# Moving half of the k and r transposes from TensorE to VectorE and DMA, with three changes to the early schedule of a recurrent-attention and SwiGLU kernel

## Chip, cores and metric

The kernel runs on one core of one Trainium2 chip, in fp32. The metric is device time in microseconds (us) of one execution, as a median over executions; lower is better. The kernel was already tuned: it takes 655.0 us, with TensorE busy for 98% of the span.

The three calls of experiments ran on three chips of the same kind (12, 8 and 2 on record). The chip of the first pair of runs is not on record; it is called the first chip below. Each call has fresh runs of the kernel before on its own chip, so times are always judged against runs of their own chip. Marks inside the traces are compared across chips too. All runs used here are in the fast state.

## The reference

Attention of the RWKV-5 kind for 4 batches, 8 heads, 768 steps and a head size of 48, followed by a SwiGLU feed-forward over 3072 tokens (384 to 1536 to 384):

```python
for t in range(S):                                   # r, k, v: (4, 8, 768, 48)
    cur = np.einsum('bhd,bhe->bhde', u[None] * kt, vt)
    y[:, :, t] = np.einsum('bhd,bhde->bhe', rt, state + cur)
    state = w[None, :, :, None] * state + np.einsum('bhd,bhe->bhde', kt, vt)
x = y.transpose(0, 2, 1, 3).reshape(B * S, H * D)    # (3072, 384)
g = x @ w_gate
out = (g * sigmoid(g) * (x @ w_val)) @ w_out
```

## The kernel before

The kernel treats attention in 24 **units** of 128 steps (six chunks of four batches). For each unit, k and r are multiplied by powers of the decay (`khat`, `rhat`, with time on the partitions), turned so that the head dimension lies on the partitions, multiplied with each other (`scores`), masked into `At`, and used for the output and for the state `Z`. The turn is done by TensorE, in eight transposes of 128x128 per unit, with ScalarE copying the PSUM results:

```python
def turn(i):
    for nm, t in (("kT", khat[i % 4]), ("rT", rhat[i % 2])):
        tp = ps_a.tile([P, HP, P], FP32, name="tp", tag="a")
        for a in range(HP):                                  # HP = 4 pairs of heads
            pe.transpose(tp[:, a, :], pair(t, a), ident[:])
        if nm == "kT":
            act.copy(kT[i % 2][:], tp[:])
        else:
            turned[i] = three.tile([P, HP, P], FP32, name=nm, tag=nm)
            act.copy(turned[i][:], tp[:])
```

Early in the kernel the weights arrive in 18 chunks and are rounded. ScalarE forms a magnitude in a PSUM bank and the low part in SBUF, VectorE combines, GpSimd adds. There is one PSUM bank for the magnitudes, used twice per chunk:

```python
def round_act(next_load=1):
    ...
    lows[n] = two.tile([P, WN], INT32, name="w_low", tag="w_low")
    for hi in halves(bits[n][:, :, 1], n):
        mag = ps_w.tile([P, WN // 2], INT32, name="w_mag", tag="w_mag")   # one bank
        ...
        act.activation(mags[n][-1].bitcast(FP32), hi.bitcast(FP32), AF.Abs, scale=float(2.0**-112))
        if len(mags[n]) == 1:
            act.activation(lows[n][:], bits[n][:, :, 0].bitcast(UINT32), AF.Copy, scale=float(2.0**-29))
            round_dve(n, 0)
    round_dve(n, 1)
```

The diagonal of `At` is written by eight small ScalarE instructions per unit, queued in `small`. One is taken with every piece of feed-forward work (`feed`), and what is left is done in a burst before the masked scores are laid over it:

```python
def feed(n):
    for _ in range(n):
        ready = [k for k, (need, _) in enumerate(todo) if need <= done["pool"] + len(summed)]
        if ready:
            todo.pop(ready[0])[1]()
        if small:
            small.popleft()()
```

The main loop (step s turns unit s, scores unit s-1, and outputs unit s-2), cut:

```python
for s in range(4, N + 2):
    ...                                # scale(s+1), own_product(s+1), loads
    if s < N:
        turn(s)
    gaps(s, 0)                         # pieces of rounding and of feed-forward
    if 4 <= s - 1 < N:
        while small:
            small.popleft()()
        scores(s - 1)
        ...
        gaps(s, 1)
    gaps(s, 2)
    ...                                # outputs(s-2), diagonal(s), update(s-2)
```

## Time and profile before

| | kernel before |
|---|---|
| median (range, runs) | 655.0 us (654.05 to 655.13, 5) |
| span of the profiled execution | 653.5 us |
| TensorE, VectorE, ScalarE, GpSimd busy | 98%, 53%, 39%, 46% |
| TensorE instructions | 4702 |
| path before 113.17 us | VectorE, ScalarE and TensorE in turn |
| path from 113.17 us to 648.06 us | matmuls only (the prediction reads its end as 647.9) |

The prediction shows the lines of the page, of the chain of waits and of the waits that this rests on. One thing that it passes over is the clock of TensorE early in the kernel: it calls the clock full, although the second digit of its own PEclk line is 8. These are two stretches of 4 us; the columns are the stretch, its length, the busy time (and instructions) of TensorE, of its weight loads, of VectorE, ScalarE and GpSimd, then the granted clock, the DMA share and GB/s.

```profile
20.00:24.00 4.00, 1.67 (x42) 1.02 (x44) 3.68 (x6) 0.94 (x2) 4.00 (x4) 0.96 0.98 197
24.00:28.00 4.00, 4.00 (x42) 3.49 (x43) 1.40 (x2) 1.84 (x3) 3.92 (x4) 0.61 1.02 386
```

TensorE is busy for only 1.67 of 4 us, and in the next stretch its clock is 0.61. The execution whose trace this is took 655.57 us at a mean clock of 0.996.

### The profile page before, as it was taken

The page shows a single profiled execution, that of the slowest core. Times are in us where ns is not written, and L with a number is a line of the kernel's source. Part 1 is how long each engine was busy: PE and PEld are TensorE (multiplying, and loading weights), DVE is VectorE, ACT ScalarE, POOL GpSimd, SP SyncE. Part 2 cuts the span into 40 slices and gives each one's busy share as a digit, 9 for nine tenths or more (in the row PEclk, how much of TensorE's full clock was granted, in tenths as well). Part 3 has the DMA queues.
Part 4 walks back from the last instruction along what each step waited for, and adds up shares of the span by engine and source line. Part 5 has one row for each costly group of instructions (what it writes and reads, how often), then busy time and mean ns, then how long its engine had stood idle before and what let it go on. Part 6 is the DMA issues. An engine that isn't in the chain of part 4 may idle for free.

```text
span 653.5 us, 11994 instructions
## 1 busy us (share of the span) xinstructions
PE 637.3 (98%) x4702; PEld 575.2 (88%) x4702; DVE 348.8 (53%) x711; ACT 257.4 (39%) x686; POOL 300.2 (46%) x333
## 2 busy tenths in 40 slices
PE   8899998999999999999999999999999999999996
PEld 8787877899988889988889988889988889988896
DVE  6668888364365556256548145546245546255460
ACT  4557776431344431344432244451244430234310
POOL 5968777961854430836416534641334310534110
PEclk9899999999999999999999999999999999999999
DMA  8969784221210010201101210000000000100001
GB/s 192 253 151 214 224 212 98 41 38 39 70 38 1 14 25 24 62 13 38 25 1 38 60 26 2 13 14 2 25 26 1 0 2 12 38 0 2 2 1 53
DMA packets 85779, 34.10 MB, mean 52 GB/s; under 512 B 76369, under 2 KB 79569, under 8 KB 85713
## 3 DMA queue, kind: packets, MB, share of 16 engines
q1 hardware_dynamic: 82256, 28.52, 19.0%
q10 hardware_dynamic: 3456, 4.72, 2.0%
q8 instruction: 39, 0.64, 0.4%
q14 instruction: 28, 0.22, 0.1%
HBM read 28.51 MB, written 4.72 MB: 51 GB/s over the span
## 4 chain that ended last, share of the span: by engine, by line
PE 86%; DVE 8%; ACT 4%; issue 1%; DMA 0%; SPq 0%; DVEq 0%; ACTq 0%
PE c_b L580 24%; PE c_a L580 20%; PE o_f L474 13%; PE o_a L474 7%; PE o_b L474 5%; PE y_ps L365 5%; PE gv L403 4%; PE s_ps L335 3%; PE tp L322 2%; PE u_ps L378 2%; ACT At L309 2%; DVE At L340 1%; DVE wo L184 1%; PE warm L245 1%; DVE hT L411 1%
## 5 line engine op out<-in xcount | busy, mean ns | idle before, releaser
L564 POOL TENSOR_TENSOR hT<-hT,u 128x256 f32<-128x256 f32 x60 | 47.3, 788 | 187.9 <-DVE hT L563 160.9
L587 ACT COPY u<-c_a 128x256 f32<-128x256 f32 x120 | 44.6, 371 | 87.0 <-PE c_a L580 86.9
L580 PE MATMUL c_a<-t,wv 128*128 128x256 f32 x240 | 72.0, 382 | 0.2 <-ACT u L587 0.2
L580 PE MATMUL c_b<-xT,wg 128*128 128x256 f32 x240 | 71.7, 380 | 0.0
L560 ACT ACTIVATE sg<-hT 128x256 f32<-128x256 f32 x120 | 50.0, 417 | 50.5 <-DVE hT L589 31.5
L309 ACT ACTIVATE At<-ident,du 128x128 f32<-128x128 f32 x184 | 64.3, 397 | 9.4 <-DVE o_sb L488 7.7
L594 DVE TENSOR_TENSOR u<-u,c_b 128x256 f32<-128x256 f32 x60 | 25.3, 421 | 70.4 <-PE c_b L580 64.1
L580 PE MATMUL c_b<-xT,s 128*128 128x256 f32 x240 | 61.6, 379 | 0.0
L589 DVE TENSOR_TENSOR hT<-p,c_b 128x256 f32<-128x256 f32 x60 | 25.2, 421 | 48.7 <-ACT u L587 24.4
L580 PEld LDWEIGHTS c_b<-xT,s 128*128 128x128 f32 x240 | 45.2, 190 | 6.6 <-DVE u L594 0.3
L540 POOL TENSOR_TENSOR s<-wv,wg 128x256 f32<-128x256 f32 x24 | 17.6, 733 | 72.4 <-PE o_f L474 57.1
L580 PEld LDWEIGHTS c_a<-t,wv 128*128 128x128 f32 x240 | 44.6, 190 | 7.1 <-ACT u L587 1.2
L580 PEld LDWEIGHTS c_b<-xT,wg 128*128 128x128 f32 x240 | 45.0, 190 | 6.1 <-issue 0.4
L340 DVE COPY_PREDICATED At<-mask,s_ps 128x512 f32<-128x512 int32 x48 | 33.0, 744 | 26.2 <-ACT At L309 16.0
L403 PE MATMUL gv<-xT,wg 128*128 128x256 f32 x144 | 36.8, 392 | 3.4 <-DVE hT L411 3.4
L365 PE MATMUL y_ps<-At,v_ld 128*32 128x128 f32 x768 | 36.1, 278 | 2.8 <-DVE At L340 2.8
L580 PE MATMUL c_b<-t,s 128*128 128x256 f32 x120 | 36.2, 383 | 0.0
L596 DVE TENSOR_TENSOR hT<-u,c_b 128x256 f32<-128x256 f32 x60 | 25.2, 421 | 20.1 <-PE c_b L580 19.9
L580 PE MATMUL c_b<-xT,wv 128*128 128x256 f32 x120 | 35.9, 381 | 0.0
L580 PE MATMUL c_a<-t,s 128*128 128x256 f32 x120 | 35.8, 380 | 0.0
L580 PE MATMUL c_a<-xT,wg 128*128 128x256 f32 x120 | 35.8, 380 | 0.0
L580 PE MATMUL c_a<-xT,wv 128*128 128x256 f32 x120 | 35.7, 379 | 0.0
(133 smaller groups left out, 1425.7 us busy)
## 6 DMA issues: line engine op xcount, KB each, us to landing
k_ld<-in_k_dram SPq DMA_DIRECT2D x24, 192.0 KB, 3.6
r_ld<-in_r_dram SPq DMA_DIRECT2D x24, 192.0 KB, 3.8
w_bits<-in_moe_w_gate_dram SPq DMA_DIRECT2D x6, 768.0 KB, 6.2
v_ld<-in_v_dram SPq DMA_DIRECT2D x48, 96.0 KB, 3.1
w_bits<-in_moe_w_val_dram SPq DMA_DIRECT2D x6, 768.0 KB, 6.5
w_bits<-in_moe_w_out_dram SPq DMA_DIRECT2D x6, 768.0 KB, 4.5
out_dram<-o_sb ACTq DMA_DIRECT2D x24, 192.0 KB, 1.9
ub<-in_u_dram SPq DMA_DIRECT2D x1, 192.0 KB, 4.1
```

The source lines that it names most:

```text
L309: lambda h=h: act.activation(At[i % 2][:, h, :], ident[:], AF.Identity, scale=du[:, h : h + 1])
L340: dve.copy_predicated(At[i % 2][:].rearrange("p (a e) t -> p a e t", e=2)[:, :, e], mask[:].bitcast(INT32).unsqueeze(1).to_broadcast([P, H ...
L365: pe.matmul(ps[32 * q : 32 * q + 32, cc, :], *x, start=start, stop=stop, skip_group_check=True,)
L403: pe.matmul(gv[:, o, :].rearrange("p (i t) -> p i t", i=2), wt[:, c, P * f : P * (f + 1)], xT[:, 2 * g % NX : 2 * g % NX + 2, c, :], start ...
L474: pe.matmul(ps, lhs[:, f, :], rhs[:, f, :], start=(f == 0 and n in (0, 1, 4)), stop=(f == FH - 1), skip_group_check=True,)
L560: act.activation(x[what, f][:], h[j], AF.Sigmoid)
L564: pool.tensor_mul(h[1], h[1], x.pop(("u3", f))[:])
L580: pe.matmul(ps.rearrange("p (i t) -> p i t", i=2), lhs, rhs, start=first, stop=what not in ("p2", "p5", "p4", "p3"), skip_group_check=True,)
L587: act.copy(x[nm, f][:], ps)
L589: dve.tensor_add(h[0], x.pop(("p1", f))[:], ps)
L594: dve.tensor_add(x["u3", f][:], x["u3", f][:], ps)
L596: dve.tensor_add(h[1], x.pop(("u2", f))[:], ps)
```

## The change

Intent: take the eight transposes of units 12 to 23 off TensorE, and shorten the early stage. In four parts.

1. **Turn on VectorE.** VectorE transposes each 32x32 block in place of the whole 128x128 array. So 16 SBUF-to-SBUF transfers per unit move the blocks to where their transposes belong, one step ahead, and two VectorE transposes of 128x512 do the rest. `khat` and `rhat` become slots of one array, `hats`, so that one transfer can take blocks of k and of r together.
2. **Room for it.** `xT` holds 10 units in place of 12, and the buffers of partial products are six in place of seven.
3. **Early, rounding and diagonals.** The two magnitudes of a chunk go to two PSUM banks (the second is `ps_o`'s, not needed until the projections). A piece of early feed-forward takes three diagonals with it in place of one.
4. **Early, order.** The masked copies of unit 1 go ahead of the rounding of the second chunk.

```diff
-    seven = ctx.enter_context(tc.tile_pool(name="seven", bufs=7))
+    six = ctx.enter_context(tc.tile_pool(name="six", bufs=6))
-    NX = 12
+    NX = 10
-    khat = [cst.tile([P, H, 64], FP32, name=f"khat{i}") for i in range(4)]
-    rhat = [cst.tile([P, H, 64], FP32, name=f"rhat{i}") for i in range(2)]
+    hats = cst.tile([P, 8, H, 64], FP32, name="hats")
+    khat, rhat = [hats[:, n] for n in (0, 2, 3, 5)], [hats[:, n] for n in (1, 4)]
+    blocks = [hats[:, n].rearrange("p h x -> p (h x)") for n in (7, 6)]
...
-            for hi in halves(bits[n][:, :, 1], n):
-                mag = ps_w.tile([P, WN // 2], INT32, name="w_mag", tag="w_mag")
+            for hi, (ps, tag) in zip(halves(bits[n][:, :, 1], n), ((ps_w, "w_mag"), (ps_o, "o"))):
+                mag = ps.tile([P, WN // 2], INT32, name="w_mag", tag=tag)
...
+    def move_blocks(i):
+        h = hats[:].rearrange("p n h x -> p (n h x)")
+        first, step = ((0, 1), (11, -1), (12, 1), (23, -1))[i % 4]
+        for m in range(4):
+            for q in range(4):
+                src = h[32 * q : 32 * q + 32, P * first + 32 * m : P * first + 32 * m + 1]
+                dst = h[32 * m : 32 * m + 32, P * 31 + 32 * q : P * 31 + 32 * q + 1]
+                sp.dma_start(...)      # 32 partitions x 8 runs of 32 floats
+
+    def turn_blocks(i):
+        turned[i] = three.tile([P, HP, P], FP32, name="rT", tag="rT")
+        for dst, src in ((kT[i % 2], blocks[0]), (turned[i], blocks[1])):
+            dve.transpose(dst[:].rearrange("p a t -> p (a t)"), src)
...
-    def feed(n):
+    def feed(n, pops=1):
...
-            if small:
+            for _ in range(min(pops, len(small))):
                 small.popleft()()
...
-                feed(1)
+                feed(1, 3)
+    BLOCKS = 12
...
     scores(0)
-    round_act()
-    round_pool()
     scores(1)
     warm(4)
     scale(2)
+    round_act()
+    round_pool()
     round_pool()
...
-        if s < N:
+        if s < BLOCKS:
             turn(s)
...
+        if BLOCKS <= s < N:
+            turn_blocks(s)
+        if BLOCKS <= s + 1 < N:
+            move_blocks(s + 1)
         gaps(s, 2)
```

More of the change, by code (lines that the diff above doesn't have):

```diff
@@ L222, in fast @@
         dve.memset(t[:, :, D:64], 0.0)
-    for t in khat + rhat:
-        dve.memset(t[:, :, D:64], 0.0)
+    dve.memset(hats[:, 0:6, :, D:64], 0.0)
     dve.memset(wcol[:], 1.0)
@@ L286, in fast, with rhat_of, at @@
     small = deque()
+    def rhat_of(i):
+        return rhat[i % 2 if i < BLOCKS else i % 4 // 2]
+    def at(i, a):
+        return HP - 1 - a if i >= BLOCKS and i % 2 == 0 else a
     def scale_k(i):
@@ L292, in scale_r @@
         for h in (slice(0, HP), slice(HP, H)) if i == 0 else (slice(0, H),):
-            pool.tensor_mul(rhat[i % 2][:, h, 0:D], r_ld[i % 2][:, h], rscale[:, h])
+            pool.tensor_mul(rhat_of(i)[:, h, 0:D], r_ld[i % 2][:, h], rscale[:, h])
     def scale(i):
@@ L327, in turn @@
                 act.copy(turned[i][:], tp[:])
+    def move_blocks(i):
[5 more added lines that the diff above has]
+                dst = h[32 * m : 32 * m + 32, P * 31 + 32 * q : P * 31 + 32 * q + 1]
+                sp.dma_start(
+                    out=bass.AP(
+                        tensor=dst.tensor, offset=dst.offset,
+                        ap=[list(dst.ap[0]), [-P, 2 * HP], [1, 32]],
+                    ),
+                    in_=bass.AP(
+                        tensor=src.tensor, offset=src.offset,
+                        ap=[list(src.ap[0]), [P * step, 2 * HP], [1, 32]],
+                    ),
+                )
+    def turn_blocks(i):
+        turned[i] = three.tile([P, HP, P], FP32, name="rT", tag="rT")
+        for dst, src in ((kT[i % 2], blocks[0]), (turned[i], blocks[1])):
+            dve.transpose(dst[:].rearrange("p a t -> p (a t)"), src)
     def scores(i):
@@ L335, in scores @@
                 pe.matmul(
-                    ps[e][:, a, :], kT[i % 2][rows, a, :], turned[i][rows, a, :],
+                    ps[e][:, a, :], kT[i % 2][rows, at(i, a), :], turned[i][rows, at(i, a), :],
                     start=True, stop=True, skip_group_check=True,
@@ L355, in outputs @@
             (cc, q), (a, s) = divmod(m, 4), divmod(m, 3)
-            each = [(z[0:R2, a, 32 * s : 32 * s + 32], rT[0:R2, a, :])] if c > 0 else []
+            each = [(z[0:R2, a, 32 * s : 32 * s + 32], rT[0:R2, at(i, a), :])] if c > 0 else []
             if s < 2:
@@ L480, in project @@
             nm = {0: "p1", 2: "u2", 3: "u3"}[n]
-            x[nm] = seven.tile([P, 2 * P], FP32, name=nm, tag="part")[:, 0:NH]
+            x[nm] = six.tile([P, 2 * P], FP32, name=nm, tag="part")[:, 0:NH]
             act.copy(x[nm], ps)
@@ L585, in four @@
             nm = {"p1": "p1", "p6": "u2", "p7": "u3"}[what]
-            x[nm, f] = seven.tile([P, 2 * P], FP32, name=nm, tag="part")
+            x[nm, f] = six.tile([P, 2 * P], FP32, name=nm, tag="part")
             act.copy(x[nm, f][:], ps)
```

## The prediction

> **What bounds the kernel now.** I read the page first: share of each engine and the forty slices.
>
> ```profile
> PE 637.3 (98%) x4702; PEld 575.2 (88%) x4702; DVE 348.8 (53%) x711; ACT 257.4 (39%) x686; POOL 300.2 (46%) x333
> PE   8899998999999999999999999999999999999996
> DVE  6668888364365556256548145546245546255460
> PEclk9899999999999999999999999999999999999999
> ```
>
> TensorE is busy nearly throughout, at full clock. But busy time of pipelined matmuls overlaps, so I went to the chain of work in order of time, which has one start after another. It falls into two parts. From 113.17 us to 647.9 us every piece is a matmul, back to back; 5.6 us of tail follow. Before 113 us, VectorE and ScalarE alternate with TensorE. The chain in a late and in an early stretch:
>
> ```profile
> 126.87 1.73 PE gv L403 x8
> 128.60 0.87 PE tp L322 x8
> 129.47 1.09 PE s_ps L335 x16
> 130.56 1.49 PE gv L403 x6
> ```
>
> ```profile
> 107.41 0.46 DVE du L217
> 107.87 0.28 DVE wo L184
> 108.24 0.57 DVE wo L185
> 108.84 0.53 ACT w_mag L166
> 109.37 1.50 ACT At L309 x5
> 111.53 0.74 DVE At L340
> 112.27 0.31 DVE sg L410
> 113.17 2.83 PE gv L403 x12
> ```
>
> The first fence shows what eight PE transposes (k and r of one unit) take on the path: 0.87 us from the first to the next work, not eight times the 273 ns that one lasts from start to end. The second shows an early step: the rounding of weights on VectorE, then a rounding op and a burst of five diagonals on ScalarE, which must be done before VectorE may lay the masked scores over them.
>
> The waits in all of 14 to 113 us put sizes on it:
>
> ```profile
> ACT w_mag L166 <- DVE wv L185: 9.3, 7, 2.1
> ACT w_mag L166 <- DVE wo L185: 8.2, 8, 1.8
> DVE At L340 <- ACT At L309: 6.2, 6, 1.3
> PE y_ps L365 <- DVE At L340: 2.8, 4, 2.1
> PE gv L403 <- DVE hT L411: 2.3, 2, 1.2
> ```
>
> ScalarE waits some 17 us in these two rows for VectorE to empty the one PSUM bank of the rounding; VectorE waits 6.2 us for diagonals.
>
> **What the Trainium skill says.** (1) "TensorE: Matmul & The Clock Gate", Part 4: PE-mode transpose, gives about 275 ns for one 128x128 transpose inside a kernel, with a PSUM result to copy. The trace agrees (median 273 ns) and its copies take 577 and 592 ns on ScalarE. (2) "VectorE: DVE Perf Modes", The three transpose paths: VectorE transposes independent 32x32 blocks; so the blocks of a 128x128 transpose must be moved by something else, here by DMA. The trace before has no such instruction. (3) "SBUF - State Buffer", Who interferes with whom: a VectorE op outside the two-port modes with one SBUF input does not contend with GpSimd, while one in such a mode blocks behind it. Consistent with the trace: the rounding's bitwise_and takes 0.35 us alone and 2.29 us at 103.68 us, beside a GpSimd add of 1.83 us. Whether a transpose escapes this the trace cannot tell; I assume it does. (4) "DMA: Bandwidth & Descriptors", Anatomy of one DMA: some 2 us of a transfer is fixed completion latency. The trace's r loads of 192 KB land 3.8 us after issue, its 0.8 KB w loads after 1.9 us, which agrees.
>
> **The change part by part.**
>
> Transposes, units 12 to 23. Removed from TensorE: 12 x 8 instructions, 12 x 0.87 = 10.4 us. The turn of unit 11 is at 128.60 us, so all twelve lie in the stretch where only matmuls are on the chain: **10.4 us gross**. ScalarE also loses 12 x (0.577 + 0.592) = 14.0 us, off the path. Added: two VectorE transposes of 128x512 per unit. As an estimate, a 128x256 add takes 421 ns and a 128x512 masked copy 745 ns here, so 0.7 us each, 1.4 us per unit, 17 us in all; a 4-byte penalty would double that. VectorE is about half busy there, so this is hidden as throughput, but not wholly as latency: a unit's pair of transposes sits in VectorE's queue between two pieces of the feed-forward. In these pieces the bank c_b is reused three matmul slots of 0.43 us (two instructions of 0.215 us) after the matmul that VectorE must read: 1.3 us, less 0.2 us latency and the 0.42 us add, leaves 0.7 us of slack. VectorE is usually idle for part of the 1.4 us, so I take 0.1 us lost per unit, about 1 us.
>
> DMA: 16 transfers per unit, each 32 partitions x 8 runs of 128 B, so 4096 runs and 512 KB. The load queue moved 82256 packets in 19.0% of 16 engines' 653.5 us, 24 ns each: 4096 x 24 / 16 = 6.2 us. Issue of a load takes SyncE 0.37 to 0.45 us when nothing holds it, so 16 take 6 to 7 us. Both overlap; with 2 us of landing a unit's move takes **8 to 10 us**. It starts after the previous unit's turn, about 40% into a step, and a late step is (458.4 - 128.6) / 12 = 27.5 us. Its reader comes a step later. Hidden. The scaling of an odd unit's r overwrites the array the move reads, at the start of the next step, some 15 us away: enough.
>
> Buffers. xT from 12 to 10 units: by program order unit i-10 was consumed two steps before, no wait. The part buffers from 7 to 6: I measured, in the trace, from the end of each GpSimd product that frees a buffer to the copy that would take it. With seven the usual margin is 2.3 us, with six 1.0 us; three of sixty are negative, -0.8 to -0.9 us, all where GpSimd scales k and r. A late copy has some 0.7 us before TensorE needs it. With the transposes adding lateness I give it 1 us in all.
>
> Late sum: 10.4 - 1 - 1 = **8.4 us**.
>
> Early stage. The most it can give is TensorE's idle time on the path. A PE-bound step (113.17 to 125.98 us) takes 12.8 us; the steps ending at 97.2 and 111.5 us have the same work and take 14.2 and 14.3 us: 1.5 us each. Counting matmuls in the other stretches gives about 1 us in 30 to 43, 1 us in 58 to 68, 0.9 us just before 113, in all 6 us after 30 us. How much comes back: in the step to 112 us VectorE itself has about 12.9 us of work, so two rounding banks and diagonals three to a piece (a burst of two in place of five) should bring 14.3 to 13.0. That recovers 1.3 x 2 + 0.7 + about 1 = 4.3 us. Unit 1 ahead of rounding: its masked copies start at 22.55 us behind 2.9 us of rounding, and TensorE waits 2.13 us for them; ahead of it they follow unit 0's at once. GpSimd now scales unit 2 first, so the turn can follow, but rounding moves 1.5 us later, and the weights' third chunk lands at 26.5 us as before. I count 1.7 of 2.5 us. **Early: 6 us.**
>
> Total 8.4 + 6.0 = 14.4 us: 655.1 - 14.4 = 640.7, called 640.5.
>
> **The rivals.**
>
> A. VectorE's latency takes the transposes' place. If one takes 1.3 us instead of 0.7, or its waits on sixteen transfers add up, each unit holds up the additions by 2.5 us and TensorE by 1 to 2 us: 12 to 20 us back, and the late part gives nothing or costs; 648 to 655. For it: additions and products alternate tightly with matmuls. Against: two masked copies (1.37 us together) already stand in that queue every step, and no TensorE wait in the late stage names them; but they are covered by 1.68 us of output matmuls, which the transposes are not.
>
> B. The moves are late, because 128-byte runs cost more than 24 ns or issue is slower. VectorE then stands in front of the transpose with all its work behind it, and GpSimd in front of the scaling, which also delays the freeing of six buffers. Above some 15 us per move this shows; at 25 us it costs several us per unit, 660 or more. Against: DMA is at 0.02 to 0.21 of its capacity in the late windows.
>
> C. The early gain does not come. The weights' loads keep DMA at 0.82 and 1.05 of its share before 40 us, and GpSimd's adds stall the bitwise_ands by 2 us wherever they meet. Then only about 8 us is left: 647.
>
> D. Nothing collides: 10.4 + 8 = 18, so 637.
>
> **Range and chances.** D sets the low end, with a little for luck: 635.5. C and half of A set the high end: 648. A gain over 2% needs 642.0 us or less, 13.1 us, so most of both parts must arrive. I give 0.62 to faster, 0.36 to within 2%, 0.02 to slower (B or a full A with C).
>
> **What would show it.** Right: tp has 96 PE instructions and its copies are 12 each, the matmuls per unit unchanged; 24 VectorE transposes near 0.7 us; 192 more DMA issues and 49152 more packets; the all-matmul stretch of the chain begins near 107 and is some 8 us shorter; w_mag no longer waits for L185, masked copies hardly for L309. Wrong in the late part: TensorE waits for VectorE additions or ScalarE copies next to the transposes, transposes of over 1 us, VectorE idle before them for a DMA. Wrong in the early part: steps still 14 us, with longer bitwise_ands beside GpSimd. A TensorE clock below 1.0 or new waits on xT would also break it.

## The result and the profile after

| | before | after |
|---|---|---|
| median (range, runs) | 655.0 us (654.05 to 655.13, 5) | 639.87 us (639.68 to 640.4, 5) |
| ratio, 95% interval | | 0.9774 (0.9761 to 0.9788): faster |
| span of the profiled execution | 653.5 us | 638.0 us |
| DMA packets | 85779 | 138003 |

A ratio in this document is the ratio of the fast runs as the record has it. It is not quite the ratio of the medians quoted.

The prediction was 640.5 us, range 635.5 to 648. The page of the changed kernel, the same four lines as the prediction shows of before:

```profile
PE 625.5 (98%) x4606; PEld 563.8 (88%) x4606; DVE 365.8 (57%) x730; ACT 244.5 (38%) x662; POOL 300.4 (47%) x333
PE   7899999999999999999999999999999999999996
DVE  6779998455356565366657355656355544355460
PEclk9999999999999999999999999999999999999999
```

TensorE has 96 instructions fewer and VectorE is busy 17.0 us longer (24 transposes in that sum). TensorE stays full in every slice but the first two and the last, so in this view whatever VectorE takes over is hidden.

The chain of waits in order of time (start, length, what):

```profile
98.53 0.48 DVE Z L426
...
99.05 1.16 PE s_ps L370 x14
100.21 2.79 PE gv L438 x12
...
111.04 0.87 PE tp L331 x8
...
630.62 1.96 PE o_b L509 x12
```

The all-matmul stretch starts at 99.05 us where before it started at 113.17. The same two ends in the chain of the kernel before:

```profile
115.99 0.87 PE tp L322 x8
...
646.10 1.96 PE o_b L474 x12
```

The piece of eight transposes at 111.04 us (before, 115.99) is the turn of unit 10. It is the same work in both kernels, so its distance of **4.95 us is what the early part brought** in these two executions. A part of that can be the clock: the trace before has the low clock from 24 to 28 us, the trace after has full clock there. Among the fresh runs of before, those with a mean clock below 0.998 were 0.8 us (first call) and 0.6 us (third call) slower than the others, and no slower in the second. The last matmuls start at 630.62 against 646.10, which is 15.48 us earlier, so the **late part brought 15.48 - 4.95 = 10.5 us**. TensorE has no wait at all after 100 us in the changed kernel's list of waits.

For the experiments one more mark is handy: the start of the first projection (`o_a`), which comes before the turn of unit 12. It is at 138.42 us before and at 133.47 after (4.95 again). From there to the end of the span it is 515.1 us before and 504.5 after. I call these the early and the late distance.

The transposes themselves. The columns are the duration in ns (lowest, median, highest), then the first and last start:

```profile
L362 DVE STREAM_TRANSPOSE kT<-hats x12: 699/711/712, 151.0 to 455.6; 128x512 f32<-128x512 f32 x12
L362 DVE STREAM_TRANSPOSE rT<-hats x12: 664/669/670, 151.7 to 456.2; 128x512 f32<-128x512 f32 x12
```

They cost what was estimated, 0.7 us. The moves are slower. The DMA issues of SyncE in the timeline (start, length, what), and GpSimd's wait for them in the list of waits (total us, times, longest):

```profile
130.11 11.22 SPq L347 DMA_DIRECT2D hats<-hats  x16
```

```profile
POOL hats L302 <- DMA hats<-hats: 24.4, 4, 7.9
```

Over the twelve moves, sixteen issues took 10.4 to 11.4 us (0.609 us for one in the median) and not 6 to 7. With 2.0 us of landing a move is 12.4 to 13.4 us and not 8 to 10. GpSimd stands four times, 24.4 us in all, in front of the scaling of r, which overwrites what the moves read; the prediction's "some 15 us away: enough" was wrong there. No engine on the chain waits for it.

The early waits, from 14 to 107 us:

```profile
ACT w_low L173 <- POOL wo L198: 3.8, 3, 2.5
ACT w_mag L169 <- DVE wv L188: 3.4, 2, 2.6
...
ACT w_mag L169 <- DVE wo L188: 0.8, 1, 0.8
...
DVE At L375 <- ACT At L318: 0.2, 1, 0.2
```

The two rows of 17.5 us in which ScalarE waited for the one bank have become 4.2 us, and VectorE's wait for diagonals went from 6.2 to 0.2 us. In exchange ScalarE, now ahead, waits for GpSimd to free the buffers of the low parts (`w_low`).

### The profile page after: what moved, and what is told of

Same layout as the page of the kernel before. It is cut to its first block, busy times and chain, and to the rows that moved or that the text cites. A ratio compares the mean times of both kernels' runs of the same rounds, so it can differ in the third digit from the quotient of the medians.

```text
span 638.0 us, 12075 instructions
## 1 busy us (share of the span) xinstructions
PE 625.5 (98%) x4606; PEld 563.8 (88%) x4606; DVE 365.8 (57%) x730; ACT 244.5 (38%) x662; POOL 300.4 (47%) x333
## 2 busy tenths in 40 slices
DMA packets 138003, 40.40 MB, mean 63 GB/s; under 512 B 128592, under 2 KB 131792, under 8 KB 137936
## 4 chain that ended last, share of the span: by engine, by line
PE 85%; DVE 8%; ACT 3%; POOL 2%; issue 1%; DMA 0%; DVEq 0%; SPq 0%; ACTq 0%; POOLq 0%
PE c_b L615 24%; PE c_a L615 20%; PE o_f L509 13%; PE o_a L509 8%; PE o_b L509 6%; PE y_ps L400 5%; PE gv L438 4%; PE s_ps L370 3%; PE u_ps L413 2%; DVE wv L187 1%; ACT At L318 1%; DVE At L375 1%; DVE wo L187 1%; DVE wv L188 1%; DVE hT L446 1%
## 5 line engine op out<-in xcount | busy, mean ns | idle before, releaser
L302 POOL TENSOR_TENSOR hats<-r_ld,rscale 128x384 f32<-128x384 f32 (+1 forms) x25 | 25.3, 1012 | 24.4 <-DMA hats<-hats 24.4
L627 DVE TENSOR_TENSOR hT<-hT,c_a 128x256 f32<-128x256 f32 x60 | 25.2, 421 | 18.6 <-PE c_a L615 17.2
```

What stands on the lines that cost most here:

```text
L302: pool.tensor_mul(rhat_of(i)[:, h, 0:D], r_ld[i % 2][:, h], rscale[:, h])
L627: dve.tensor_mul(h[0], h[0], ps)
```

## The experiments

My theory after the result: the late part is TensorE time that nobody else had to pay for (10.4 us), and the early part is as predicted, from banks, diagonals and order together. Rivals: the late gain comes from ScalarE's freed time (24 copies fewer) and not from TensorE; the early gain comes from one part alone; VectorE's transposes and the moves do cost something, and something else hides it. "After" in a label means the changed kernel.

### First call: the parts, TensorE's work put back, and an earlier start

**late_only** is the changed kernel with parts 3 and 4 undone. **early_only** is the kernel before with parts 3 and 4:

```diff
 late_only (from the changed kernel)
-            for hi, (ps, tag) in zip(halves(...), ((ps_w, "w_mag"), (ps_o, "o"))):
+            for hi in halves(...):                     # one bank
...
-                feed(1, 3)
+                feed(1)
...
     scores(0)
+    round_act(); round_pool()
     scores(1); warm(4); scale(2)
-    round_act(); round_pool()
     round_pool()
```

> The changed kernel with its three early parts taken back (one PSUM bank for the rounding, unit 1's copies behind the rounding, one diagonal per piece); transposes of units 12 to 23 by VectorE and the smaller buffers stay. Theory (the twelve turns are worth the whole of their TensorE time, 12 x 0.87 = 10.4 us, as the two traces suggest: 15.5 us in all, of which 5.0 had come by the transposes of unit 10): 655.0 - 10.4 = 644.6, at the same granted clock. Rival (the parts need each other: without the early parts the late one gives less, as ScalarE's and VectorE's queues come later to unit 12): 647 or more. My prediction on record said 8.4 us: 646.6.

> The kernel before with the three early parts alone; all turns stay on TensorE, buffers as before. Theory: the first transposes of unit 10 start about 5 us earlier (115.99 us before, 111.04 us in the changed kernel) and nothing changes behind them: 655.0 - 5.0 = 650.0. Prediction on record: 6.0 us, 649.0. Rival (part of what shows before unit 10 comes from the move to VectorE or from the layout of the arrays): 651.5 or more.

Measured, beside 655.61 us of before on this chip: late_only 645.16 us (644.08 to 645.43, 5 runs), ratio 0.9837 (0.9824 to 0.9849), so 10.45 us less; its late distance is 505.0 us, that of before 515.1. early_only 653.51 us (651.42 to 655.05, 17 runs), ratio 0.9969 (0.9961 to 0.9978), so only 2.1 us less, with a spread of 3.6 us that goes with the mean granted clock of the execution: 651.42 us at 0.999, 654.29 at 0.992, 655.05 at 0.993. So the late part stands alone at its full size. The early part's best execution is 4.2 us under the median of before (2.8 us under the best of before), its median half of that, and something in it moves the clock. So the theory for early_only (650.0) was missed, and its rival's number was met, though the times go with the clock and nothing here points to the rival's reason, the move to VectorE.

**pe_back** is the changed kernel with eight TensorE transposes per unit put back in front of VectorE's; their results are not read, and ScalarE does not copy them:

```diff
     def turn_blocks(i):
+        for t in (khat[i % 4], rhat_of(i)):
+            tp = ps_a.tile([P, HP, P], FP32, name="tp", tag="a")
+            for a in range(HP):
+                pe.transpose(tp[:, a, :], pair(t, a), ident[:])
```

> The changed kernel, which in units 12 to 23 also does the eight TensorE transposes as before, into a PSUM bank that nothing reads (no ScalarE copies; the result is unchanged). Theory (what the late part saves is the TensorE time alone): 639.9 + 10.4 = 650.3. Rival (a good part of the gain is ScalarE's freedom from its 24 copies, 14 us of work, or PSUM banks held for shorter): clearly less comes back, 645 or less.

Measured: 651.54 us (650.51 to 653.17, 6), ratio 0.9940 (0.9926 to 0.9953). Its late distance is 514.8 us against 504.5 after, and against 505.0 in late_only, which has the same late code on the same chip: **the twelve times eight transposes cost 9.8 to 10.3 us**, 0.82 to 0.86 us per unit. ScalarE still lacks its 24 copies here, and yet the late distance is within 0.3 us of that of before (515.1). The rival of ScalarE's freed time falls.

**from_10** starts VectorE's turn at unit 10, where a step lasts 12.6 us in place of 27:

```diff
-    khat, rhat = [hats[:, n] for n in (0, 2, 3, 5)], ...
+    khat, rhat = [hats[:, n] for n in (3, 5, 0, 2)], ...
...                                                        # rhat_of follows
-        first, step = ((0, 1), (11, -1), (12, 1), (23, -1))[i % 4]
+        first, step = ((12, 1), (23, -1), (0, 1), (11, -1))[i % 4]
...
-    BLOCKS = 12
+    BLOCKS = 10
```

> The changed kernel with VectorE turning from unit 10 on instead of 12 (the k and r arrays are assigned to units two further on, so that a unit's two arrays stay neighbours). In the changed kernel the chain is matmuls alone from 99.05 us on, and the turns of units 10 and 11 start at 111.04 and 123.65 us. Theory (any turn inside that stretch is worth 0.87 us): 639.9 - 1.7 = 638.1. Rival (so early VectorE is still full with rounding, and its transposes push the masked copies): no gain or a loss, 640 to 642.

Measured: 646.10 us (642.73 to 647.50, 5), ratio 0.9851 (0.9829 to 0.9873). `o_a` starts at 133.37 us, 1.7 us earlier than in pe_back on the same chip (135.07; the turns of unit 9 start within 0.02 us of each other), which is the TensorE time of two more turns. But the late distance is 510.2 us, against 504.5 after and 505.0 in late_only: over 5 us lost. The timeline shows how:

```profile
123.74 11.45 SPq L347 DMA_DIRECT2D hats<-hats  x16
```

```profile
136.52 0.71 DVE L362 STREAM_TRANSPOSE kT<-hats 128x512 f32<-128x512 f32 x1 [6.90 <-DMA hats<-hats]
```

```profile
142.82 2.98 PE L509 MATMUL o_a<-wt,hs 128*128 128x192 f32 x12 [1.90 <-DVE hs L483]
```

The move takes 11.45 us to issue; VectorE sits idle for 6.90 us in front of the transpose, with all its other work behind it; then TensorE waits 1.90 us for one of VectorE's sums. An earlier wait for VectorE, at 138.74 us, is 1.27 us long. In the next stretch (144 to 148 us) the granted clock is 0.57, which costs some 1.7 us (an estimate: 4 us at 0.57). Together that is 4.9 us of the loss. This is the prediction's rival B. It is real, and the changed kernel escapes it because its steps (27 us) are twice as long as the move.

### Second call: which early part, and the clock

**after_again** is the changed kernel unaltered, on another chip. **order_alone** is the kernel before with part 4 only. **banks_diag** is the kernel before with part 3 only. **after_warm** is the changed kernel with ten matmuls on a tile of their own put before the turn of unit 3.

```diff
 after_warm
     round_act(0)
+    ps = ps_a.tile([P, HP, P], FP32, name="fill", tag="a")
+    for _ in range(10):
+        pe.matmul(ps[:, 0, :], ident[:], ident[:], start=True, stop=True)
     turn(3)
```

> The changed kernel, unaltered, on the chip of this call. In the first call's chip the early parts alone gave 651.4 to 655.1 us, with granted clocks of 0.999 down to 0.992; its trace shows the clock at 0.50 from 32 to 34 us, behind a pause of TensorE of 2.0 us for the scaling of r of unit 3. Theory (this pause sometimes costs the clock for some 4 us): the changed kernel too has executions of two kinds, about 640 at a clock of 1.0 and 642 to 643 at 0.994 or so, and the time goes with the clock. Rival (the early parts alone lack something that the whole has): all executions at 639.5 to 640.5.

> The kernel before with unit 1's masked copies, and the scaling of unit 2, ahead of the rounding; nothing else. Prediction on record: 1.7 us from this part. In the traces the scores of unit 2 start at 33.42 us before and at 31.43 us changed: 2.0 us. It also removes TensorE's 2.1 us pause at 21 us, behind which the clock stood at 0.61 from 24 to 28 us. Theory: these 2.0 us last to the end, as the steps behind it are of fixed length: 653.0, in executions at full clock. Rival (the next steps are bound by VectorE and the loads of weights and take it back): 654.5 to 655.

> The kernel before with two PSUM banks for the rounding and three diagonals per early piece, the order of unit 1 as before. Theory (in the traces the distance from the scores of unit 2 to those of unit 10 is 83.38 us before and 80.42 us changed, so these two parts are worth 3.0 us and the order 2.0 us): 652.0. Prediction on record: 4.3 us, 650.7. Rival (all of the early gain needs the order): 654 or more.

> The changed kernel with ten idle-filling matmuls (identity by identity, into a PSUM tile that nothing reads, 1.1 us) ahead of the turn of unit 3, where TensorE pauses for 1 to 2 us. Theory (the pause costs the clock): no execution with a clock below 0.998 from this place, so 640 at most on any chip; where the changed kernel runs at full clock anyway, no difference (within 0.5 us). Rival (the clock falls from another pause, or by chance): the same spread as the changed kernel of this call.

| kernel | us (range, runs) | over before (655.75 us) | `o_a` starts | late distance |
|---|---|---|---|---|
| after_again | 643.26 (641.38 to 643.50, 5) | 0.9803 (0.979 to 0.9816) | 136.72 | 504.8 |
| order_alone | 658.12 (655.86 to 658.5, 6) | 1.0030 (1.0018 to 1.0042) | 140.59 | 515.6 |
| banks_diag | 651.82 (651.36 to 652.48, 5) | 0.9943 (0.9931 to 0.9956) | 133.47 | 516.0 |
| after_warm | 643.03 (641.74 to 644.20, 5) | 0.9798 (0.9785 to 0.981) | 137.39 | 505.0 |

**The order of unit 1 is worth nothing, and here it costs.** banks_diag, without the new order, reaches the first projection at 133.47 us, exactly where the full change did; the clock is 1.00 until there in both traces. By the times it gains 3.9 us. The order by itself is 2.4 us slower than before.

Why it is worth nothing even at full clock is seen in TensorE's waits (14 to 113 us). In banks_diag, with the old order, the wait for the masked copies is there:

```profile
PE y_ps L365 <- DVE At L340: 3.2, 4, 2.4
```

In the changed kernel it has shrunk, but others stand in its place:

```profile
PE tp L331 <- POOL hats L298: 1.0, 1, 1.0
PE y_ps L400 <- ACT kT L333: 0.8, 1, 0.8
PE tp L331 <- POOL hats L302: 0.6, 1, 0.6
PE s_ps L370 <- DVE Z L426: 0.6, 1, 0.6
PE y_ps L400 <- DVE At L375: 0.6, 2, 0.3
```

The wait for the masked copies fell from 3.2 to 0.6 us; the waits for GpSimd's scaling and for Z went from 0.3 to 2.2 us. The pause moved from 20 to 24 us (unit 1) to 28 to 32 us (unit 2).

Why it costs is late weights and the clock. In after_again the pause at 28 to 32 us is followed by a low one (columns as above):

```profile
28.00:32.00 4.00, 2.06 (x13) 1.33 (x11) 3.34 (x7) 3.37 (x8) 3.52 (x4) 1.00 0.79 263
32.00:36.00 4.00, 3.48 (x19) 3.08 (x19) 2.67 (x6) 4.00 (x12) 3.45 (x3) 0.51 1.13 287
36.00:40.00 4.00, 4.00 (x15) 3.06 (x15) 3.07 (x6) 0.92 (x3) 2.46 (x2) 0.64 1.03 176
```

By these lines the clock is at half for some 6.8 us, by which TensorE loses some 3.4 us (an estimate). `o_a` is 136.72 - 133.47 = 3.25 us late, but that is not the clock alone. pe_back has the same code up to there and a similar pause, at a clock of 1.00 throughout, and its `o_a` is at 135.07 us. So by these single executions 1.6 us come with the late weights and their pause, and 1.65 us with the clock. The timeline says what made the pause; a bracket gives the idle time just before and what ended it:

```profile
28.41 0.52 ACT L169 ACTIVATE w_mag<-w_bits 128x384 f32<-128x384 f32 x1 [5.07 <-DMA w_bits<-in_moe_w_gate_dram]
...
30.81 1.11 PE L331 MATMUL tp<-ident,hats 128*128 128x128 f32 x8 [1.86 <-ACT kT L333]
```

ScalarE stood 5.07 us in front of a rounding op whose weights had not landed. The copy of unit 2's k stood behind that op in ScalarE's queue, the PSUM bank of that turn stayed taken, and TensorE waited 1.86 us for it at the next turn. On the first chip the same chunk let ScalarE go on at 25.47 us, not 28.41, and no such wait appears. That was early: in all other kept traces, the trace before included, it is 26.56 to 28.54 us.

The old order is not free of this. Its pause, at 20 to 24 us, is followed by a clock of 0.50 from 24 to 26 us in the traces of before, late_only and banks_alone (1.00 in those of banks_diag and no_order). But in the trace before this lasts some 3.4 us, half as long as here.

Five executions of after_again on this chip: 641.38 us at a mean clock of 0.999, and 642.82 to 643.50 us at 0.992 to 0.993. The dip comes by execution. Even the fastest is 1.5 us above the first chip's 639.87, and the ratio of 0.979 to 0.9816 leaves open whether the change gains 2% on this chip. In early_only, pe_back and from_10 the times also spread over 2.7 to 4.8 us; pe_back and from_10 show a similar pause in their profiled execution, without a dip. So a pause makes a dip possible; the traces do not say what decides.

**after_warm** was to fill the pause and keep the clock up. The median did not change: its own tile waited 2.2 us for the very bank that was late, so the matmuls came after the pause, and the clock was 0.50 under them from 31 to 34 us. A miss of the experiment, not of the idea.

### Third call: the order undone, the pause filled, the transposes doubled, the banks alone

```diff
 no_order (from the changed kernel): the order as before
     scores(0)
+    round_act(); round_pool()
     scores(1); warm(4); scale(2)
-    round_act(); round_pool()
     round_pool()

 after_fill: 16 matmuls on the tile that warm(4) already has, so no new bank is needed
-    warm(4)
+    last = warm(4)
...
     round_act(0)
+    for _ in range(16):
+        pe.matmul(last[:, 0, 0:P], ident[:], ident[:], start=True, stop=True)
     turn(3)

 turn_twice: VectorE does each transpose two times
-            dve.transpose(dst[:].rearrange("p a t -> p (a t)"), src)
+            for _ in range(2):
+                dve.transpose(dst[:].rearrange("p a t -> p (a t)"), src)

 banks_alone (from the kernel before)
-            for hi in halves(...):
+            for hi, (ps, tag) in zip(halves(...), ((ps_w, "w_mag"), (ps_o, "o"))):
```

> The changed kernel with unit 1's copies and the scaling of unit 2 back behind the rounding; two banks, three diagonals and the late transposes stay. In the last call the order alone made the kernel before slower by 2.4 us (clock 0.993), banks and diagonals gave 3.9 us. Theory (the order moves TensorE's pause from 21 us to 29 us, where on most chips it costs the clock for 4 to 8 us; the late part adds its 10.4 us to anything): 651.8 - 10.4 = 641.4, with little spread, and under the changed kernel's 643.3 of that chip. Rival (order and the rest need each other): 643 or more.

> The changed kernel with sixteen idle-filling matmuls (1.7 us) ahead of the turn of unit 3, written into the PSUM tile of the last warming matmuls. The first try at this waited itself 2.2 us for a PSUM buffer (its ten matmuls had a tile of their own in the pool of the transposes), so it filled nothing. Theory (the pause at 29 us costs the clock): full clock from 28 to 44 us, and 640.0 to 641.4 in all executions. Rival (the pauses for the r array and the scores behind it, 0.8 and 0.6 us, suffice for the loss): as the changed kernel on most chips, 643.

> The changed kernel with each of VectorE's 24 transposes done twice (same result): 2.76 us in VectorE's queue per unit in place of 1.38. This is the size that rival A of the prediction assumed: TensorE then loses 1 to 2 us per unit, 12 to 24 us in all. Theory from the trace of the changed kernel (no TensorE wait at all after 100 us, so there is slack left, but how much it does not show): 0.3 to 1 us per unit, 4 to 12 us over the changed kernel (641 to 643 on these chips). If nothing is lost at all, latency on VectorE's queue was never a danger at this place and the 0.1 us per unit of the prediction was a guess on the wrong side.

> The kernel before with two PSUM banks for the rounding and nothing else. Banks and diagonals together gave 3.9 us. Theory (the banks take away ScalarE's 21 us of waiting, but the burst of five diagonals stays ahead of the masked copies, so VectorE gains only its 3.8 us of waits for the second rounding op, of which some 1.5 to 2 us in the steps that are on the chain): 653.5 to 654.3. Rival (ScalarE, freed of its wait, is ahead in the burst too, so the diagonals are worth nothing more): 652.

| kernel | us (range, runs) | over before (655.39 us) | `o_a` starts | late distance |
|---|---|---|---|---|
| no_order | 640.92 (640.69 to 641.44, 5) | 0.9784 (0.9771 to 0.9797) | 133.76 | 505.1 |
| after_fill | 641.35 (640.57 to 642.53, 5) | 0.9790 (0.9776 to 0.9803) | 134.57 | 504.9 |
| turn_twice | 647.62 (646.12 to 648.52, 4) | 0.9877 (0.9862 to 0.9892) | 136.37 | 510.4 |
| banks_alone | 652.11 (651.91 to 652.58, 5) | 0.9954 (0.994 to 0.9968) | 135.29 | 515.0 |

**no_order** gives the whole gain without part 4, and five runs within 0.75 us. The unaltered changed kernel was not run on this chip, so it is not shown that no_order beats it. (turn_twice has its early code; its `o_a` is 2.6 us later than here, in an execution with the dip.) The ratio of no_order, 0.9784, lies between the 0.9774 that the full change reached at full clock and the 0.9803 where the clock fell.

**after_fill** keeps the clock. Its weights were late too (ScalarE waited 4.98 us, until 27.89 us), yet TensorE was busy through the stretch and the clock stayed up, here and in the stretch after; its five runs have a mean clock of 0.998 to 1.0.

```profile
28.00:32.00 4.00, 4.00 (x36) 3.95 (x35) 3.69 (x8) 3.71 (x9) 3.52 (x4) 1.00 0.81 245
```

An unfilled run beside it on this chip is turn_twice, whose code is that of the changed kernel up to the turn of unit 12. In its trace ScalarE waited 4.85 us for the same chunk, until 27.73 us; TensorE was busy for 1.61 us from 28 to 32 us, and the clock was 0.51 in the next 4 us and 0.64 in the 4 us after. Its `o_a` is at 136.37 us, 1.8 us later than that of after_fill. Two of its four executions have a mean clock of 0.994 and 0.996, none of the five of after_fill is below 0.998. That fits the account of the pause. So few executions do not settle it, as the dip also stays out of unfilled ones; and two of the five times (641.52 and 642.53 us) lie above the 641.4 that the theory allowed.

**turn_twice** asks whether the 1.38 us of transposes per unit are free because VectorE has room, or nearly too much. The second 1.38 us cost: the late distance grows from 504.9 and 505.1 us (after_fill and no_order, on this chip) to 510.4 us, some 5.4 us or 0.45 us per unit. TensorE's waits from 140 us on name VectorE's additions and a copy of ScalarE, as rival A had them:

```profile
PE c_b L616 <- DVE hT L625: 2.7, 2, 1.4
PE c_a L616 <- ACT u L623: 0.9, 1, 0.9
```

Named waits are 4.1 us in all (these and 0.5 us at an `o_f`). So A's mechanism exists, at a third of what A asked per unit (1 to 2 us), and it begins somewhere between once and twice the load that the change puts on. (The time of 647.62 us also holds an early clock dip: `o_a` is late, at 136.37.)

**banks_alone** gains 3.3 us by the times, which is its rival's number, and 138.42 - 135.29 = 3.1 us at `o_a`. Of the 3.9 us of banks_diag that leaves some 0.6 us by the times for three diagonals per piece. This is not clear of noise: the intervals of the two ratios (0.9931 to 0.9956 and 0.994 to 0.9968) overlap. At `o_a` it is 1.8 us, but there the trace of banks_alone has the low clock from 24 to 28 us and that of banks_diag has not. The late distance of banks_diag (516.0 and not 515.1) is no loss of TensorE: from the start of its last `o_b` matmuls to the end of the span it takes 8.5 us, and 7.4 to 7.6 us in the other traces compared. Why is not known.

## Why the prediction was right

| term of the sum | predicted us | measured us | by |
|---|---|---|---|
| 96 TensorE transposes off the path | -10.4 | -9.8 to -10.6 | late_only, pe_back, late distances |
| VectorE's latency in the late pieces | +1 | 0 | late distance, no TensorE wait after 100 us |
| six part buffers | +1 | 0 | no wait on them |
| two banks and three diagonals | -4.3 | -3.9 (times), -5.0 (at `o_a`, partly clock) | banks_diag |
| order of unit 1 | -1.7 | 0 at full clock, +2.4 alone | banks_diag, order_alone |
| sum | -14.4 | -15.1 (the terms, by times, add to -13.7 to -14.5) | result |

- **What bounds the kernel** was read rightly. The late stage is matmul after matmul, so TensorE time taken away there comes off the time one to one. pe_back is the cleanest proof, since it takes back the 9.8 to 10.3 us with ScalarE and VectorE unchanged.
- **The late deductions** were too careful by 2 us. The transposes lasted 0.71 and 0.67 us as estimated; the doubling by "a 4-byte penalty" did not come. That they do not contend with GpSimd, which the prediction assumed, agrees with the trace: the pair at 200.55 us, beside GpSimd's work, took 0.70 and 0.67 us. The first 1.38 us per unit cost nothing and the second 0.45 us, so the slack was there and ends before twice the load.
- **The step that failed** is "I count 1.7 of 2.5 us" for unit 1's masked copies ahead of the rounding. The wait that it removes was real (2.1 us), but a pause is only gained if nothing else is due just after. Unit 2's turn was: it now waits for GpSimd's scaling and for a PSUM bank. The prediction had seen the two facts that decide ("rounding moves 1.5 us later, and the weights' third chunk lands at 26.5 us as before") and took only 0.8 us off for them. The sum was right because this error and the late deductions cancel, which is luck; so is it that the first pair met early weights and a full clock (643.26 us on the second call's chip).
- **The size of a move** was wrong: 10.4 to 11.4 us of issue, not 6 to 7. "Issue of a load takes SyncE 0.37 to 0.45 us when nothing holds it" was read from the first issue of a series; the trace before also has the second of a series, 0.58 us for r just after k, and sixteen in a row are like the second. It did no harm in 27 us steps. from_10 shows that it does in steps of 12.6 us.
- **Packets** grew by 52224, predicted 49152. DMA issues (192), `tp` (96) and its copies (12 each) were as said. Early, the wait for diagonals nearly vanished as said; the `w_mag` waits fell from 17.5 to 4.2 us. Waits on `xT` did not appear. The all-matmul stretch was to begin near 107 us and be some 8 us shorter; it begins at 99.05 us and is only 1.4 us shorter (533.5 against 534.9 us), as more of the early steps are now matmuls alone.
- **A citation**: the section on one DMA that the prediction names describes the path through GpSimd, and these transfers are issued by SyncE. The 1.9 and 2.0 us of landing stand by the traces. The page's 275 ns for a transpose are for bf16, and the 273 ns here for fp32.
- **The clock** was named as something that could break the prediction, but only in general. With the landing of the weights it is what spreads the changed kernel's median from 639.87 us on one chip to 643.26 on another (0.9774 and 0.9803 of before), as far as single traces show.

Left open: what decides whether a pause brings a dip, when the weights land, and whether no_order or a filled pause beats the change as it is on a chip where the dip occurs.

## What to carry to other kernels

In a stage where the chain is one engine's work back to back, moving work off that engine pays its full time, provided that the receiver's latency fits between its other work; test that by doubling the moved work, which shows how much slack is left. Time a series of DMA issues by the second of two in a row, and compare the whole move with the length of the step that hides it. A wait that is removed early in a pipeline is only a gain if the next item of the engine is not waiting for the same late producers, so look at what is due right behind it, and at the granted clock of the stretch after each pause.

## What the Trainium skill lacked or had wrong

- "TensorE: Matmul & The Clock Gate", Part 1, What's actually happening: its table ties the half clock to an idle window of some 3.4 us and the text says that the moment varies. In after_warm the clock was 0.50 from 31 to 34 us after one pause of 2.20 us, with TensorE busy in the 4 us before it. In pe_back and from_10 pauses of 1.80 and 1.65 us, with a second of 0.65 and 0.83 us soon after, kept 1.00; in after_again 1.86 and 0.60 us were followed by 0.51. The variation agrees; a full idle window as the condition does not. The page's section on PSUM-queue cycling allows for shorter gaps, but gives no length.
- "VectorE: DVE Perf Modes", The three transpose paths: it has one figure, 311 ns for 128x128 in bf16. In fp32 one instruction over 128x512 took 0.711 us (k) and 0.669 us (r), nearly constant over 24 (699 to 712 and 664 to 670 ns), a quarter of which per 128x128 is 0.17 to 0.18 us.
- "DMA: Bandwidth & Descriptors", Anatomy of one DMA: it puts sequencer dispatch at some 50 ns for the path through GpSimd. For a copy issued by another sequencer the page has only 512 cycles per instruction, for the generations before trn3, and no time for a series. Here one such SBUF-to-SBUF issue of 256 runs occupied SyncE for 0.609 us, and sixteen for 10.4 to 11.4 us, which was the larger part of the move. Landing took 2.0 us, which agrees with its fixed cost.
- No page works through how a late weight load acts on TensorE through ScalarE's queue: an op waiting 5.07 us for DMA held the PSUM copy behind it, TensorE then waited 1.86 us for the bank, and the first projection came 3.25 us later, with the lower clock that followed.
